# Half of the second layer's weights decoded during the first phase and kept in DRAM; the first batch's x @ w_in by token tile

## The chip, the core and the metric

The kernel runs on one core of a Trainium2 chip. Its engines are TensorE (PE, matmuls; its weight loads stand apart as PEld), VectorE (DVE), ScalarE (ACT), GpSimd (POOL) and SyncE (SP, which here only issues the DMAs). The metric is device microseconds (us) of one execution. Three runs of the kernel before the change took 1190.75, 1192.31 and 1192.62 us, so the median is 1192.31.

## The reference

```python
# attention over 8 batches x 8 heads: 512 tokens and 32 state rows per head, D = 64
scores  = x @ state.T / 8;  a  = softmax(scores);   xread = a @ state
scores2 = state @ x.T / 8;  a2 = softmax(scores2);  sread = a2 @ x
x = concat([xread, sread], tokens)      # heads joined: 8 * (512 + 32) = 4352 rows of 512
# first layer, 512 -> 1024 -> 512
h = x @ w_in;  solu = h * softmax(h)
ln = (solu - mean) / sqrt(var + 1e-6) * g_ln
y = ln @ w_out
# second layer, 512 -> 2048 -> 512
g = relu(y @ w2_in) ** 2
out = g @ w2_out
```

The weights come as float64. The kernel reads them as pairs of 32-bit words and turns each pair into a float32 on the chip. A matmul of full precision is then made of three passes with operands split into a high and a low part (`PASSES`): high x high, high x low, low x high.

## The kernel before, in words

**Two phases.** Phase one takes the eight batches b = 0 to 7 in turn: attention, `x @ w_in`, the SoLU with its layer norm, and `ln @ w_out`, whose result goes to DRAM (`y_d`). After batch 7 the state rows of all batches follow as one group "s" of 256 rows (lines 839 to 844). Phase two reads the `y_d` back group by group (`load_y`) and computes for each of 16 slices m of the 2048 hidden columns a product L3 (`emit_l3`, output `h`), the relu and square (`relu2`), and a product L4 (`emit_l4`, output `o`). L4 of a slice stands two slices behind its L3 (`LAG = 2`).

**What runs ahead.** While PE multiplies batch b by w_out (`emit_l2`, eight slices k, output `y`), it also does attention of batch b + 2 and `x @ w_in` of batch b + 1 (`emit_l1`), placed between the column tiles by the `after` table. For each slice k it transposes the normed tokens (`emit_lnT`, output `lnTp`); ACT and DVE turn them into the high and the low part of `lt` (lines 644 and 647), which the products of that slice read. `emit_lnT` of slice k + 1 stands ahead of the products of slice k.

**Decoding a weight.** `decode` (line 263) makes one 128x512 block of float32 out of 512 KB: a DMA from SP into one of three `raw` buffers, an ACT instruction (Prelu, line 291), two DVE instructions (shift and shift-or, lines 294 and 297) in one of three `dec` buffers, then in `split_w` an ACT cast to the high part (line 241) and a subtraction for the low part on POOL or DVE (line 247). w_in has eight such blocks, w_out eight, and the second layer 32: for each slice m one of w2_in (`wa`) and one of w2_out (`wb`). `load_w2(m)` starts both. Slices 0 to 3 start at k = 4 to 7 of batch 7, slices 4 to 7 at every second k of group "s", slices 8 to 15 at the start of phase two.

**First batch.** w_in is decoded by halves of its columns c = 0, 1. `emit_sw(0, c)` multiplies the state by the half c, and `emit_l1(0, t)` (four token tiles t) needs `sw` of a half for its products of that half. The four tiles are written as generators: the program takes the half c = 0 of all four tiles first, then `emit_sw(0, 1)`, then the half c = 1 of all four (lines 764 to 774).

**What sets the order.** Nothing is reordered on the chip: each engine takes its instructions in the order in which the program emits them. That order comes from `Flow`, a small planner with a clock of its own. Every piece of work off PE is a generator that offers its next step with the engines that may do it, a cost for each and the time from which it is ready; `poll` hands a step out as soon as an engine is free by the planner's costs, the task with the earliest latest-start first. The program is built twice, and the second time the due times that the first found (`plan`) set these priorities.

Of the kernel before, what the change touches and what calls it, by code (L numbers as in the profile page):

```python
# [8 lines left out]
F32 = mybir.dt.float32  # L9
# [139 lines left out]
def attn_solu_relu2_kernel(  # L149
# [58 lines left out]

    y_d = [dram.tile([P, KD, S], F32, name=f"y_d{b}") for b in range(B)]
    y_ds = dram.tile([P, KD, NSR], F32, name="y_ds")  # L210

    wi = [ap_.tile([P, F1], F32, name=f"wi{k}") for k in range(KD)]
    wo = [wp.tile([P, 2, DM], F32R, name=f"wo{k}") for k in range(K1)]
# [11 lines left out]
    def take(name):  # L225
        def ok():
            if room[name]:
                room[name] -= 1
                return True
        return None, 0.0, ok  # L230
# [32 lines left out]
    def decode(dst_h, dst_l, src, pool=None, w=None, spare=False):  # L263

        raw, dec = ("raw2", "dec2") if spare else ("raw", "dec")
        if pool is None:  # L270
            yield take(raw)
            t = (ap_ if spare else raw_p).tile(
                [P, 512, 2], I32, tag=raw, name="raw", bufs=3
            )
        else:
            t = pool.tile([P, 512, 2], I32, tag="u", name="raw_u")
        tf = t.rearrange("p n c -> p (n c)")
        src = src.bitcast(I32)
        if len(src.shape) == 3:
            tf = tf.rearrange("p (k f) -> p k f", k=src.shape[1])  # L280
        f = dma(tf, src, 512)
        own = w is None
        if own:
            yield take(dec)
            w = (ap_ if spare else dec_p).tile(
                [P, 512], F32, tag=dec, name="dec", bufs=2 if spare else 3
            )
        w_i = w.bitcast(I32)
        hi, lo = t[:, :, 1], t[:, :, 0]
        h = hi.bitcast(F32)  # L290
        f = yield {"A": 0.66}, f, lambda e: nc.scalar.activation(
            out=w, in_=h, func=AF.Prelu, scale=2.0 ** -112, alpha=-(2.0 ** 32)
        )
        f = yield {"V": 0.46}, f, lambda e: nc.vector.tensor_scalar(  # L294
            out=w_i, in0=w_i, scalar1=3, scalar2=None, op0=ALU.logical_shift_left
        )
        f = yield {"V": 0.69}, f - fl.HOP, lambda e: nc.vector.scalar_tensor_tensor(  # L297
            out=w_i, in0=lo, scalar=29, in1=w_i, op0=ALU.logical_shift_right, op1=ALU.bitwise_or
        )
        if pool is None:  # L300
            give(raw)
        if not own:
            return f
        f = yield from split_w(dst_h, dst_l, w, f)
        give(dec)
        return f
# [67 lines left out]
    def exp_t(b, g):  # L374


        et = e_T[b, g] = ap_.tile([P, S], F32, tag="eT", name="eT", bufs=1)
        task = done.pop(("nm", b, g))
        s, nm, l = s_sb[b][:, g, :], nms.pop((b, g)), l2[b][:, g:g + 1]

        def gen():
            yield None, 0.0, lambda: task["done"] is not None
            f = yield {"A": 0.82}, task["done"], lambda e: nc.scalar.activation(
                out=et, in_=s, func=AF.Exp, bias=nm, accum_out=l
            )
            return f

        done["eT", b, g] = fl.spawn(gen(), 3.0)
# [44 lines left out]
    def emit_e(b, g):  # L433


        ps = pm.tile([P, T, P], F32, tag="m", name="ep")
        fl.pe(0.11 * T, pm_slot(), done.pop(("eT", b, g)))
        et = e_T.pop((b, g))
        for t in range(T):
            nc.tensor.transpose(ps[:, t, :], et[:, t * P:(t + 1) * P], ident)  # L440
        done["e2", b, g] = one(
            {"A": 0.6, "V": 0.65}, copy(s_sb[b][:, g, :], ps.rearrange("p t q -> p (t q)"))
        )
        pm_free.append(done["e2", b, g])

    def emit_aT(b, g):
        f = fl.need(done["a", b, g])
        if g == 0:
            aT[b] = ap_.tile([P, 2, G, S], F32R, tag="aT", name="aT")
        ps = pm.tile([P, T, P], F32, tag="m", name="aTp")  # L450
        fl.pe(0.11 * T, f, pm_slot())
        for t in range(T):
            nc.tensor.transpose(ps[:, t, :], a_sb[b][:, g, t, :], ident)  # L453
        pf = ps.rearrange("p t q -> p (t q)")
        if b == 0:
            done["aT", b, g] = one({"A": 0.57, "V": 0.6}, copy(aT[b].bitcast(F32)[:, 0, g, :], pf))
        else:
            done["aT", b, g] = split_psum(aT[b][:, 0, g, :], aT[b][:, 1, g, :], pf, 512)
        pm_free.append(done["aT", b, g])
# [158 lines left out]
    def emit_l1(b, t, in_y=False):  # L618
        a, w, passes = aT[b], sw[b], PASSES
        if b == 0:  # L620
            a, w, passes = a.bitcast(F32), w.bitcast(F32), ((0, 0),)
        return solu_ln(b, t, l1_products(
            in_y, [done["aT", b, g] for g in range(G)], lambda c: done["sw", b, c],
            lambda i, k: a[:, i, k, t * P:(t + 1) * P], lambda j, k: w[:, j, k], G, passes,
        ))
# [76 lines left out]
    def phase2_right():  # L702
# [4 lines left out]
        p2["o"] = ctx.enter_context(tc.tile_pool(name="op", bufs=3, **right, **tw))  # L707
        w2_tiles(p2["w"], 0, K2 // 2)

    def load_w2(m):  # L710
        src = w2_in[:, m * P:(m + 1) * P].rearrange("(k p) f -> p k f", p=P)
        done["wa", m] = fl.spawn(decode(wa[m][:, 0], wa[m][:, 1], src))
        done["wb", m] = fl.spawn(decode(wb[m][:, 0], wb[m][:, 1], w2_out[m * P:(m + 1) * P, :]))

    def load_y(j):
        src, n = groups[j]
# [43 lines left out]
    emit_sw(0, 0, True)  # L760
    for g in range(G):
        emit_aT(0, g)
    exp_t(0, 0)
    l1_0 = [emit_l1(0, t, t % 2 == 0) for t in range(T)]
    for i, h in enumerate(l1_0):
        if i % 2:
            emit_e(0, i // 2)
            if i < T - 1:
                exp_t(0, i // 2 + 1)
        if i == T - 1:  # L770
            emit_sw(0, 1, True)
        next(h)
    for h in l1_0:
        next(h)
    sread(0)
    load_xn(1)
    scores(1)
# [6 lines left out]

    emit_lnT(0, 0, T)

    for b in range(B):
        nxt, nn = b + 1 < B, b + 2 < B
        off = 1 if b == 0 else 0
        l1_at = [t + (b < 2) for t in range(T)]  # L790
        if b == 0:
            load_x(2)
        for k in range(K1):
            if k + 1 < K1:
                emit_lnT(b, k + 1, T)
            after = {c: [] for c in range(KD)}
            if b == 0 and k == 0:
                after[1].append(lambda: emit_aT(1, 0))
                after[3].append(lambda: emit_aT(1, 1))
            if b == 0 and k == 1:  # L800
                after[1].append(lambda: sread(b + 1))
                after[3].append(lambda: emit_xs(b + 1))
                if nn:
                    after[1].append(lambda: load_xn(b + 2))
            if nn:
                if k == off + 1:
                    after[1].append(lambda: scores(b + 2))
                    if b + 3 < B:
                        after[3].append(lambda: load_x(b + 3))
                for g in range(G):  # L810
                    if k == off + 3 + g:
                        after[2].append(lambda g=g: emit_e(b + 2, g))
                for g in range(G):
                    if k == off + 2 + g:
                        after[2].append(lambda g=g: (emit_sT(b + 2, g), exp_t(b + 2, g)))
                if k >= 6:
                    after[3].append(lambda: emit_sw(b + 2, k - 6))
                if k >= 6:
                    after[1].append(lambda: emit_aT(b + 2, k - 6))
            if b >= 1 and nxt and k == 0:  # L820
                after[3].append(lambda: emit_xs(b + 1))
            if b == B - 1:
                if k in (0, 2):
                    after[3].append(lambda: run(emit_l1s(k // 2)))
                if k == 3:
                    phase2_right()
                    load_y(0)
                if k >= 4:
                    load_w2(k - 4)
            if k == K1 - 1:  # L830
                after[1].append(lambda: emit_lnT(*((b + 1, 0, T) if nxt else ("s", 0, TS))))
            emit_l2(b, k, T, y_d[b], after)
            if k in l1_at and nxt:
                run(emit_l1(b + 1, l1_at.index(k)))
        if nn:
            sread(b + 2)
            if b + 3 < B:
                load_xn(b + 3)
    for k in range(K1):
        if k + 1 < K1:  # L840
            emit_lnT("s", k + 1, TS)
        emit_l2("s", k, TS, y_ds)
        if k % 2:
            load_w2(4 + k // 2)
    p1.close()


# [131 lines left out]
```

## Time and profile before

| | |
|---|---|
| median of three runs | 1192.31 us |
| the profiled execution | 1192.82 us |
| its span, first to last instruction | 1190.8 us |
| PE busy | 1148.4 us (96%) |
| DVE busy | 546.5 us (46%) |
| ACT busy | 492.6 us (41%) |
| POOL busy | 167.7 us (14%) |
| DMA | 71.22 MB, mean 60 GB/s |
| mean granted clock of TensorE | 0.988 |

The profiled execution takes 2.0 us more than its span, and it is 0.5 us above the median. Times on the rows below count from the start of the span. The shares of busy time are means over stages that differ: the start, up to the first products with w_out at about 60 us; the eight batches, to 411 us; group "s", to 432 us; phase two behind it, whose first 74 us still decode weights.

### The profile page before, as it was taken

The numbers are of one execution on the slowest core, as the hardware profiler recorded it, in microseconds if no ns is written. First come the engines' busy times: TensorE is split into PE (matmuls) and PEld (weight loads), VectorE is DVE, ScalarE is ACT, GpSimd is POOL, SyncE is SP. The second block draws the span as 40 slices with busy tenths as digits, with TensorE's granted clock in tenths as the row PEclk, the third lists the DMA queues.
The fourth block names the chain that finished last, engine by engine and source line by source line (L and its number), as shares of the span: only waits on it lengthen the run. The fifth ranks groups of instructions, "written<-read, shape, count | busy, mean of one in ns | idle before, by whom it ended". The sixth has DMA issues, their size and how long they took to land.

```text
span 1190.8 us, 14915 instructions
## 1 busy us (share of the span) xinstructions
PE 1148.4 (96%) x5992; PEld 912.7 (77%) x5992; DVE 546.5 (46%) x873; ACT 492.6 (41%) x875; POOL 167.7 (14%) x210
## 2 busy tenths in 40 slices
PE   5699999999999988899999999999999999999998
PEld 2377777777777766688888888888888888888887
DVE  6866766766753589723223223233223233232222
ACT  5856766666754566523222223222222232232222
POOL 1521311311322345200000000000000000010000
PEclk9899999999999999899999999999999999999999
DMA  9323032131002366302002011010020020010000
GB/s 361 119 78 114 1 113 78 36 113 72 1 37 89 109 209 198 120 1 71 1 7 65 1 26 45 1 40 32 1 68 4 1 71 1 1 54 1 1 36 18
DMA packets 27701, 71.22 MB, mean 60 GB/s; under 512 B 3312, under 2 KB 12528, under 8 KB 25584
## 3 DMA queue, kind: packets, MB, share of 16 engines
q1 hardware_dynamic: 27632, 70.27, 17.4%
q8 instruction: 47, 0.77, 0.3%
q14 instruction: 22, 0.18, 0.0%
HBM read 52.43 MB, written 17.83 MB: 59 GB/s over the span
## 4 chain that ended last, share of the span: by engine, by line
PE 86%; DVE 6%; DMA 4%; ACT 2%; issue 2%; SPq 0%; ACTq 0%; DVEq 0%
PE o L897 29%; PE h L882 29%; PE y L673 14%; PE hps L612 8%; PE lnTp L638 2%; DMA raw<-w_out 2%; DVE dec L297 1%; DMA raw<-w_in 1%; PE hps L358 1%; DVE dec L294 1%; DMA raw_u<-w_in 1%; PE srd L469 1%; DVE u L577 1%; PE sTp L397 1%; PE aTp L453 1%
## 5 line engine op out<-in xcount | busy, mean ns | idle before, releaser
L897 PE MATMUL o<-wb,g 128*128 128x512 f32 x1632 | 398.9, 392 | 6.8 <-DVE g L247 4.5
L882 PE MATMUL h<-yt,wa 128*128 128x512 f32 (+1 forms) x1728 | 395.3, 378 | 0.0
L897 PEld LDWEIGHTS o<-wb,g 128*128 128x128 f32 x1632 | 306.7, 189 | 73.4 <-DVE g L247 6.9
L882 PEld LDWEIGHTS h<-yt,wa 128*128 128x128 f32 x1728 | 314.5, 189 | 61.6
L866 DVE TENSOR_TENSOR r<-r 128x512 f32<-128x512 f32 (+1 forms) x144 | 109.0, 757 | 386.0 <-ACT r L859 385.8
L859 ACT ACTIVATE r<-h 128x512 f32<-128x512 f32 (+1 forms) x144 | 82.7, 574 | 397.5 <-PE h L882 397.5
L673 PE MATMUL y<-lt,wo 128*128 128x512 f32 (+1 forms) x864 | 221.1, 397 | 8.0 <-DVE lt L647 5.9
L673 PEld LDWEIGHTS y<-lt,wo 128*128 128x128 f32 x864 | 149.8, 190 | 46.6 <-issue 8.4
L247 DVE TENSOR_TENSOR g<-r,g 128x512 fp32r<-128x512 f32 (+1 forms) x144 | 96.3, 669 | 80.8 <-ACT g L241 74.9
L241 ACT CAST g<-r 128x512 fp32r<-128x512 f32 (+1 forms) x144 | 85.8, 596 | 100.2 <-DVE r L866 99.6
L612 PE MATMUL hps<-sw,aT 128*128 128x512 f32 x368 | 97.5, 413 | 0.5 <-ACT sw L241 0.5
L247 POOL TENSOR_TENSOR yt<-yraw,yt 128x1024 fp32r<-128x1024 f32 (+1 forms) x8 | 18.2, 2276 | 551.7 <-ACT yt L241 551.7
L612 PEld LDWEIGHTS hps<-sw,aT 128*128 128x128 f32 x368 | 68.6, 189 | 22.6 <-issue 5.6
L548 DVE TENSOR_REDUCE hm<-hps 128x1 f32<-128x512 f32 x68 | 46.3, 690 | 51.7 <-PE hps L612 46.1
L647 DVE SCALAR_TENSOR_TENSOR lt<-lnTp,g_sb,lt 128x512 fp32r<-128x512 f32 (+1 forms) x72 | 51.6, 718 | 32.5 <-ACT lt L644 31.8
L241 ACT COPY u<-hps 128x512 f32<-128x512 f32 x68 | 39.7, 583 | 62.9 <-DVE hm L548 62.9
L591 POOL TENSOR_SCALAR es<-es 128x1 f32<-128x1 f32 x34 | 30.4, 893 | 191.3 <-ACT e L572 190.3
L644 ACT ACTIVATE lt<-lnTp,g_sb 128x512 fp32r<-128x512 f32 (+1 forms) x72 | 48.3, 673 | 8.2 <-PE lnTp L638 8.2
L577 DVE SCALAR_TENSOR_TENSOR u<-u,e 128x1024 f32<-128x1024 f32 x34 | 46.4, 1365 | 10.3 <-ACT e L572 10.2
L583 ACT ACTIVATE e<-u,nmu 128x1024 f32<-128x1024 f32 x34 | 39.2, 1153 | 20.5 <-DVE nmu L580 20.5
L638 PE MATMUL lnTp<-ident,u 128*128 128x128 f32 x272 | 42.4, 276 | 3.5 <-POOL u L601 2.5
L638 PEld LDWEIGHTS lnTp<-ident,u 128*128 128x128 f32 x272 | 33.4, 142 | 12.0 <-POOL u L601 2.7
(82 smaller groups left out, 714.0 us busy)
## 6 DMA issues: line engine op xcount, KB each, us to landing
raw<-w_out SPq DMA_DIRECT2D x24, 512.0 KB, 4.5
out<-osb SPq DMA_DIRECT2D x34, 256.0 KB, 2.2
xT<-x_t SPq DMA_DIRECT2D x8, 1024.0 KB, 4.8
xn<-x_n SPq DMA_DIRECT2D x8, 1024.0 KB, 5.4
y_d<-ys SPq DMA_DIRECT2D x16, 512.0 KB, 2.7
yraw<-y_d SPq DMA_DIRECT2D x16, 512.0 KB, 5.7
raw<-w_in SPq DMA_DIRECT2D x16, 512.0 KB, 4.1
raw_u<-w_in SPq DMA_DIRECT2D x8, 512.0 KB, 9.5
```

Source lines behind the costliest of these rows:

```text
L241: nc.scalar.copy(out=out, in_=in_)
L247: return lambda e: eng_of[e].tensor_tensor(out=out, in0=in0, in1=in1, op=ALU.subtract)
L577: nc.vector.scalar_tensor_tensor(out=u, in0=u, scalar=1.0, in1=e_, op0=ALU.mult, op1=ALU.mult, accum_out=us)
L612: nc.tensor.matmul(out=ps, lhsT=lhsT(i, k), rhs=rhs(j, k)[:, cs], start=(k == 0 and n == 0), stop=(k == n_k - 1 and n == len(passes) - 1),)
L638: nc.tensor.transpose(ps[:, t, :], u_t[key, t][:, k * P:(k + 1) * P], ident)
L644: f = yield {"A": 0.1 + nt * 0.143}, f, lambda e: nc.scalar.activation(out=o[:, 0], in_=pf, func=AF.Copy, scale=gk)
L647: f = yield {"V": 0.1 + nt * 0.155}, f, lambda e: nc.vector.scalar_tensor_tensor(out=o[:, 1], in0=pf, scalar=gk, in1=o[:, 0].bitcast(F32), ...
L673: nc.tensor.matmul(out=ps, lhsT=wo[k][:, w, c * P:(c + 1) * P], rhs=o[:, a], start=(k == 0 and i == 0), stop=(k == K1 - 1 and i == 2),)
L859: first = one({"A": 0.06 + n / 1000}, lambda e: nc.scalar.activation(out=r, in_=hps, func=AF.Relu))
L866: f = yield {"V": 0.15 + n / 960}, first["done"], lambda e: nc.vector.tensor_tensor(out=r, in0=r, in1=r, op=ALU.mult)
L882: nc.tensor.matmul(out=hps, lhsT=wa[m][:, w, k, :], rhs=yt[j][:, a, k, :], start=(k == 0 and i == 0), stop=(k == KD - 1 and i == 2),)
L897: nc.tensor.matmul(out=ops[j][t], lhsT=g[:, a, t * P:(t + 1) * P], rhs=wb[m][:, w, :], start=(m == 0 and i == 0), stop=(m == K2 - 1 and i ...
```

## The change

There are two edits. First, the 16 blocks of slices 0 to 7 of the second layer are decoded during batches 1 to 6, at k = 0, 3 and 6, into one of three buffers (`w2s`, with the tag of buffers that the decoding of w_out no longer needs) and stored to 16 new DRAM tiles `w2_d`. From k = 4 of batch 7 on, `reload_w2` brings them back with 16 plain DMAs into `wa` and `wb`. The decoding in batch 7 and in group "s" is gone; slices 8 to 15 are decoded where they were. Second, `emit_sw(0, 1)` stands ahead of the first batch's `emit_l1`, and each token tile runs through both halves before the next one starts.

```diff
+    w2_d = [dram.tile([P, 2, 512], F32, name=f"w2_d{i}") for i in range(K2)]
...
+    def early_w2(i):
+        def gen():
+            yield take("raw2")
+            t = ap_.tile([P, 2, 512], F32R, tag="raw2", name="w2s", bufs=3)
+            src = w2_sources(i // 2)[i % 2]
+            th, tl = t[:, 0], t[:, 1]
...
+            yield from decode(th, tl, src)
+            dma(w2_d[i], t.bitcast(F32), 512)
+            give("raw2")
+        done["w2_d", i] = fl.spawn(gen(), 30.0)
+    def reload_w2(m):
+        fl.need([done["w2_d", 2 * m], done["w2_d", 2 * m + 1]])
+        done["wa", m] = dma(wa[m].bitcast(F32).rearrange("p a k f -> p a (k f)"), w2_d[2 * m], 512)
+        done["wb", m] = dma(wb[m].bitcast(F32), w2_d[2 * m + 1], 512)
...
+    emit_sw(0, 1, True)
     exp_t(0, 0)
-    l1_0 = [emit_l1(0, t, t % 2 == 0) for t in range(T)]
-    for i, h in enumerate(l1_0):
-        if i % 2:
-            emit_e(0, i // 2)
-            if i < T - 1:
-                exp_t(0, i // 2 + 1)
-        if i == T - 1:
-            emit_sw(0, 1, True)
-        next(h)
-    for h in l1_0:
-        next(h)
+    for t in range(T):
+        run(emit_l1(0, t, t % 2 == 0))
+        if t % 2:
+            emit_e(0, t // 2)
+            if t < T - 1:
+                exp_t(0, t // 2 + 1)
...
                 if k >= 4:
-                    load_w2(k - 4)
+                    reload_w2(2 * k - 8)
+                    reload_w2(2 * k - 7)
+            if b in range(1, 7) and k % 3 == 0 and early:
+                early_w2(early.pop(0))
...
         emit_l2("s", k, TS, y_ds)
-        if k % 2:
-            load_w2(4 + k // 2)
```

The line numbers of the changed kernel are 2 higher in the functions around the change, and 25 higher in phase two.

PE at the start, before: `aTp` are the transposed attention weights of batch 0, `hps<-sw,aT` the products of `emit_l1`, `hps<-wi` those of `emit_sw`, `ep` transposes for the state read, `srd` the state read.

```order
L453 MATMUL aTp<-ident,a_sb 128x128 x8
L612 MATMUL hps<-sw,aT 128x512 x2
L440 MATMUL ep<-ident,eT 128x128 x4
L612 MATMUL hps<-sw,aT 128x512 x4
L440 MATMUL ep<-ident,eT 128x128 x4
L358 MATMUL hps<-wi_106,bdf 32x512 x2
L358 MATMUL hps<-wi_107,bdf 32x512 x2
L358 MATMUL hps<-wi_108,bdf 32x512 x2
L358 MATMUL hps<-wi_109,bdf 32x512 x2
L612 MATMUL hps<-sw,aT 128x512 x10
L469 MATMUL srd<-xn,s_sb 32x64 x32
```

The same place of PE in the changed kernel:

```order
L455 MATMUL aTp<-ident,a_sb 128x128 x8
L360 MATMUL hps<-wi_122,bdf 32x512 x2
L360 MATMUL hps<-wi_123,bdf 32x512 x2
L360 MATMUL hps<-wi_124,bdf 32x512 x2
L360 MATMUL hps<-wi_125,bdf 32x512 x2
L614 MATMUL hps<-sw,aT 128x512 x8
L442 MATMUL ep<-ident,eT 128x128 x4
L614 MATMUL hps<-sw,aT 128x512 x8
L442 MATMUL ep<-ident,eT 128x128 x4
L471 MATMUL srd<-xn,s_sb 32x64 x32
```

The eight products with the second half of w_in moved ahead of all sixteen products of the four token tiles; before, six of the sixteen stood ahead of them.

DVE in a middle batch, before: from the high and low part of one slice (`lt`) over the lines of attention (`aT`, `sw`) to the next.

```order
L647 SCALAR_TENSOR_TENSOR lt<-lnTp,g_sb,lt 128x512
L601 TENSOR_SCALAR u<-u,nmu,vs 128x1024
L647 SCALAR_TENSOR_TENSOR lt<-lnTp,g_sb,lt 128x512
L601 TENSOR_SCALAR u<-u,nmu,vs 128x1024
L247 TENSOR_TENSOR aT<-aTp,aT 128x512
L247 TENSOR_TENSOR sw<-hps,sw 128x512 x2
L247 TENSOR_TENSOR aT<-aTp,aT 128x512
L647 SCALAR_TENSOR_TENSOR lt<-lnTp,g_sb,lt 128x512
```

The same stretch of DVE in the changed kernel:

```order
L649 SCALAR_TENSOR_TENSOR lt<-lnTp,g_sb,lt 128x512
L603 TENSOR_SCALAR u<-u,nmu,vs 128x1024
L649 SCALAR_TENSOR_TENSOR lt<-lnTp,g_sb,lt 128x512
L249 TENSOR_TENSOR aT<-aTp,aT 128x512
L296 TENSOR_SCALAR dec<-dec 128x512
L299 SCALAR_TENSOR_TENSOR dec<-raw,dec 128x512
L249 TENSOR_TENSOR sw<-hps,sw 128x512 x2
L249 TENSOR_TENSOR aT<-aTp,aT 128x512
L649 SCALAR_TENSOR_TENSOR lt<-lnTp,g_sb,lt 128x512
```

The two instructions of one decode came in ahead of the `sw` and the second `aT`, and one `u` went to POOL.

DVE at the end of group "s" and the start of phase two, before: each 128x256 `lt` of a slice stands behind a decode; `r` and `g` are the square and the low part of `relu2`.

```order
L647 SCALAR_TENSOR_TENSOR lt<-lnTp,g_sb,lt 128x256
L294 TENSOR_SCALAR dec<-dec 128x512
L297 SCALAR_TENSOR_TENSOR dec<-raw,dec 128x512
L647 SCALAR_TENSOR_TENSOR lt<-lnTp,g_sb,lt 128x256
L294 TENSOR_SCALAR dec<-dec 128x512
L297 SCALAR_TENSOR_TENSOR dec<-raw,dec 128x512
L294 TENSOR_SCALAR dec<-dec 128x512
L297 SCALAR_TENSOR_TENSOR dec<-raw,dec 128x512
L294 TENSOR_SCALAR dec<-dec 128x512
L297 SCALAR_TENSOR_TENSOR dec<-raw,dec 128x512
L866 TENSOR_TENSOR r<-r 128x512
```

The same place of DVE in the changed kernel:

```order
L649 SCALAR_TENSOR_TENSOR lt<-lnTp,g_sb,lt 128x256 x8
L891 TENSOR_TENSOR r<-r 128x512
L249 TENSOR_TENSOR g<-r,g 128x512
L296 TENSOR_SCALAR dec<-dec 128x512
L299 SCALAR_TENSOR_TENSOR dec<-raw,dec 128x512
L891 TENSOR_TENSOR r<-r 128x512
L296 TENSOR_SCALAR dec<-dec 128x512
L299 SCALAR_TENSOR_TENSOR dec<-raw,dec 128x512
L249 TENSOR_TENSOR g<-r,g 128x512
```

The eight `lt` of group "s" follow one another with no decode between them, and the decodes of slices 8 to 15 begin behind the first square of phase two.

## Rows read from the trace of the kernel before

**Rows 1.** Windows of stages: length, busy us (instructions) per engine, PEclk, DMA share, GB/s.

```profile
0.00:60.30 60.30, 38.13 (x244) 16.35 (x244) 47.82 (x91) 43.94 (x82) 21.56 (x34) 0.89 0.63 237
...
411.40:431.70 20.30, 14.85 (x112) 13.14 (x111) 15.99 (x23) 13.49 (x28) 10.94 (x8) 1.00 0.68 224
431.70:505.40 73.70, 66.94 (x267) 52.16 (x266) 60.23 (x74) 42.87 (x73) 29.55 (x21) 0.93 0.54 170
505.40:1190.80 685.40, 681.73 (x3097) 567.82 (x3095) 201.80 (x288) 176.40 (x295) 18.18 (x8) 1.00 0.08 24
```

**Rows 2.** Timeline of PE, end of phase one: start, us, what, [idle before it <- releaser].

```profile
388.58 7.03 PE L612 MATMUL hps<-wi,xs 128*128 128x512 f32 x16
...
412.15 1.96 PE L673 MATMUL y<-lt,wo 128*128 128x256 f32 x12 [0.35 <-ACT lt L644]
...
414.09 1.63 PE L673 MATMUL y<-lt,wo 128*128 128x256 f32 x12
...
415.69 1.66 PE L673 MATMUL y<-lt,wo 128*128 128x256 f32 x12
...
431.69 8.34 PE L882 MATMUL h<-yt,wa 128*128 128x512 f32 x36
```

**Rows 3.** Timeline of PE, first part of phase two.

```profile
465.07 2.56 PE L897 MATMUL o<-wb,g 128*128 128x512 f32 x10 [1.37 <-DVE g L247]
...
494.64 4.64 PE L897 MATMUL o<-wb,g 128*128 128x512 f32 x10 [0.61 <-DVE g L247]
...
505.37 0.84 PE L882 MATMUL h<-yt,wa 128*128 128x512 f32 x3
```

**Rows 4.** Chain that ended last, undisturbed phase two: start, us, what.

```profile
502.81 2.72 PE o L897 x12
```

**Rows 5.** Tile dec from 404 to 500 us: shortest/median/longest in ns.

```profile
L291 ACT ACTIVATE dec<-raw x32: 657/668/710, 403.9 to 493.2; 128x512 f32<-128x512 f32 x32
L294 DVE TENSOR_SCALAR dec<-dec x32: 411/422/1523, 405.4 to 494.5; 128x512 int32<-128x512 int32 x32
L297 DVE SCALAR_TENSOR_TENSOR dec<-raw,dec x32: 691/693/1810, 406.1 to 495.0; 128x512 int32<-128x512 int32 x32
L241 ACT CAST wa<-dec x16: 602/619/628, 407.7 to 482.1; 128x512 fp32r<-128x512 f32 x16
...
L247 POOL TENSOR_TENSOR wa<-dec,wa x15: 1286/1410/1803, 408.4 to 481.3; 128x512 fp32r<-128x512 f32 x15
```

**Rows 6.** Timeline of DVE, phase two with decoding.

```profile
453.02 1.78 DVE L866 TENSOR_TENSOR r<-r 128x512 f32<-128x512 f32 x1
...
456.77 0.68 DVE L247 TENSOR_TENSOR g<-r,g 128x512 fp32r<-128x512 f32 x1
...
468.24 1.59 DVE L866 TENSOR_TENSOR r<-r 128x512 f32<-128x512 f32 x1
```

**Rows 7.** Windows: one middle batch, columns as in rows 1.

```profile
190.30:235.60 45.30, 44.57 (x315) 33.98 (x314) 30.74 (x57) 29.36 (x55) 9.95 (x18) 1.00 0.22 75
```

**Rows 8.** Line 647 (low part of lt): shortest/median/longest in ns.

```profile
L647 DVE SCALAR_TENSOR_TENSOR lt<-lnTp,g_sb,lt x72: 472/750/753, 59.5 to 429.9; 128x512 fp32r<-128x512 f32 x64, 128x256 fp32r<-128x256 f32 x8
```

**Rows 9.** Timeline of PE, the one wait of a middle batch.

```profile
222.77 0.66 PE L397 MATMUL sTp<-ident,s_sb 128*128 128x128 f32 x4 [0.73 <-ACT s_sb L241]
```

**Rows 10.** Timeline of PE, the start.

```profile
22.02 2.37 PE L612 MATMUL hps<-sw,aT 128*128 128x512 f32 x4
...
32.15 7.13 PE L612 MATMUL hps<-sw,aT 128*128 128x512 f32 x16 [0.53 <-ACT sw L241]
39.22 1.10 PE L469 MATMUL srd<-xn,s_sb 128*32 128x64 f32 x64
...
60.26 2.08 PE L673 MATMUL y<-lt,wo 128*128 128x512 f32 x4 [2.14 <-DVE lt L647]
```

**Rows 11.** Timeline of ACT, the exponential of the first batch's last token tile.

```profile
48.48 1.14 ACT L572 ACTIVATE e<-u,nmx 128x1024 f32<-128x1024 f32 x1
```

**Rows 12.** Windows: a stretch full of weight loads, columns as in rows 1.

```profile
10.00:20.00 10.00, 5.38 (x24) 1.61 (x23) 9.30 (x20) 6.25 (x11) 1.05 (x1) 0.98 1.02 419
```

More of the change, by code (lines that the diff above doesn't have):

```diff
@@ L708, in phase2_right, with w2_sources @@
         w2_tiles(p2["w"], 0, K2 // 2)
-    def load_w2(m):
-        src = w2_in[:, m * P:(m + 1) * P].rearrange("(k p) f -> p k f", p=P)
-        done["wa", m] = fl.spawn(decode(wa[m][:, 0], wa[m][:, 1], src))
-        done["wb", m] = fl.spawn(decode(wb[m][:, 0], wb[m][:, 1], w2_out[m * P:(m + 1) * P, :]))
+    def w2_sources(m):
+        return (
+            w2_in[:, m * P:(m + 1) * P].rearrange("(k p) f -> p k f", p=P),
+            w2_out[m * P:(m + 1) * P, :],
+        )
+    def load_w2(m):
+        a, b = w2_sources(m)
+        done["wa", m] = fl.spawn(decode(wa[m][:, 0], wa[m][:, 1], a))
+        done["wb", m] = fl.spawn(decode(wb[m][:, 0], wb[m][:, 1], b))
+    def early_w2(i):
[4 more added lines that the diff above has]
+            th, tl = t[:, 0], t[:, 1]
+            if i % 2 == 0:
+                th, tl = (v.rearrange("p (k f) -> p k f", k=KD) for v in (th, tl))
+            yield from decode(th, tl, src)
[6 more added lines that the diff above has]
+        done["wb", m] = dma(wb[m].bitcast(F32), w2_d[2 * m + 1], 512)
     def load_y(j):
@@ L785, in attn_solu_relu2_kernel @@
     emit_lnT(0, 0, T)
+    early = list(range(K2))
     for b in range(B):
```

## The prediction

> **What bounds the kernel now.** I read the windows by stage first. PE sets the time wherever it is busy throughout, so the question for each stage is what PE loses there. Behind 505 us it loses next to nothing: 681.7 of 685.4 us busy at full clock. The losses are in three places [rows 1]: the start, where DVE is busy 47.8 of 60.3 us and PE only 38.1; group "s", where PE is busy 14.9 of 20.3 us; and the first 74 us of phase two, where PE is busy 66.9 us and its granted clock is 0.93 in the mean, between its two levels of 1.2 and 2.4 GHz. In the last two DVE is busy 16.0 of 20.3 and 60.2 of 73.7 us, and the decoding of w2 is what it has there beside its steady work.
>
> Two timelines of PE give these two losses in numbers. In group "s" the second slice starts at 414.09 and the third at 415.69, so an undisturbed slice takes 1.60 us. Seven such steps from the second slice on would end at 414.09 + 7 x 1.60 = 425.29. Phase two starts at 431.69 instead [rows 2]: 6.4 us lost, and 0.35 before the first slice, where `lt` waits on an ACT queue that holds decoding. That is 6.8. In phase two one product of 12 matmuls takes 2.72 us [rows 4]. From 431.69 to 505.37 PE does 264 matmuls (36 at first, then ten products with w2_out and nine with w2_in), 22 x 2.72 = 59.8 us of work in 73.7 us [rows 2, 3]. So 13.8 us are lost there, part of it to waits (1.37, 0.61 us) and part to clock: ten matmuls take 2.56 us behind one wait and 4.64 behind the longer ones near 494 [rows 3]. Both stages together lose 20.6 us.
>
> **Group "s".** The change takes every decode out of batch 7 and group "s", and the eight `lt` follow one another on DVE. The reload takes no time of ACT, DVE or POOL. It is 16 DMAs of 512 KB, 8.4 MB. At the 419 GB/s of a stretch full of loads that is 20 us [rows 12]; at the 224 of group "s" 37 us [rows 1]. The space for it is free when the last products with w_in end, at 388.58 + 7.03 = 395.6 [rows 2], 29 us before phase two would now start (near 424.8), and slice m needs 1 MB every 5.44 us, which is 4.7 us of transfer even at the lower rate. So it is hidden, with slice 0 first in the queue. The stores of `y_d` stand behind it on SP; they are read again only in the last group but one of phase two. The gain is 6.8 us, with 6.4 and 7.1 (eight steps of 1.60 from 411.8 on) as its ends.
>
> **Phase two.** Sixteen blocks are still decoded, and DVE's order has three decodes per slice m, as before. What such a step takes is in the trace: from the square at 453.02 to that at 468.24 there are two steps with three decodes each, 7.61 us a step [rows 6]. PE needs 5.44 us a step. By the shortest durations the step would be 3 x (0.42 + 0.69) + 0.69 + 0.68 = 4.7 us [rows 5, 6], and would fit. The row shows instead that the shift and the shift-or reach 1.52 and 1.81 us while POOL subtracts for 1.41 [rows 5]. The Trainium skill, page "SBUF — State Buffer", section "Who interferes with whom", says that a DVE instruction with two SBUF inputs and a GpSimd instruction that reads SBUF share a port that one of them holds for its whole instruction. By that rule the stretched steps stay, since 14 of the 16 subtractions are again on POOL; the trace agrees. By the shortest durations nothing would be lost in this stage (a rival below).
>
> I replay it with 7.61 us a step. Count from the start S of phase two. The first three products with w2_in end at 2.7, 5.4 and 8.2 us. The first decodes wait for their DMAs (issued about S, landing 4 to 5 us later), so the squares of slices 0 to 2 are hardly held up: slice 2 has its square near 9.5. Then comes the pace of three decodes a step: squares 3, 4, 5 near 16.5, 24.1, 31.7; square 6, with a `yt` subtraction in its step, near 40. The low part `g` is done 4.4 us behind its square (456.77 + 0.68 - 453.02, [rows 6]): 20.9, 28.5, 36.1, 44.4. PE wants them at 24.5, 29.9, 35.4 and 40.8 (slice m at 8.16 + 5.44m). Slices 3 and 4 are in time, slice 5 is late by less than the first two passes of its product, which need the high part alone, and slice 6 by about 3.5 us. Behind it the last decode is done and the delay shrinks. I add 1 us for matmuls at the lower clock behind that wait, so 4.5 of the 13.8 us remain and 9.3 come back. The ends: 13.8, if DVE keeps up, and 13.8 - 11.6 = 2.2, if the 16 decodes cost their whole excess, 16 / 3 x (7.61 - 5.44) = 11.6 us.
>
> **Batches 1 to 6.** Each of 16 early decodes adds ACT 0.67 + 0.62 = 1.29 us, DVE 0.42 + 0.69 = 1.11 us, POOL 1.41 us [rows 5], and on SP two DMAs of 512 KB. That is 2.7 decodes a batch: 3.4 us of ACT and 3.0 of DVE, against 45.3 - 29.4 = 15.9 and 45.3 - 30.7 = 14.6 us that these two have idle [rows 7]. So on the mean they are covered, and what counts is what queues behind a decode. PE waits for `lt` alone with little to spare, and on DVE the decodes stand in the stretches where products of `emit_l1` give PE more to do, and beside `aT` and `sw`; none stands directly between the tight `lt` of the last slices. `lt` itself never stretches: 0.753 us at most in 72 [rows 8]. The one wait that PE has in a batch, 0.73 us for the copy of `ep` on ACT [rows 9], can grow. On SP the store of a decoded block waits for POOL, and the loads of x behind it have most of a batch to spare. Per decode the ends are 0 and 1.29 + 1.11 = 2.40 us, fully exposed; over 16 that is 0 to 38. I take 1.0 us in all, nearest to a wait of 0.73 that grows by a quarter in each of six batches.
>
> **The start.** Before, the products of the first half begin at 22.02, while the second half is still being decoded; the last eight run from 32.15 to 39.22, 0.89 us each (16 records, two to a product) [rows 10]. Now all sixteen stand behind the second half. At the worst they begin where that half's products began before: 32.15 + 16 x 0.89 + 2 x 0.6 for the two `ep` = 47.6, 8.4 us after 39.22. But the exponential of the last tile ran only at 48.48 [rows 11], some 8 us after its product could have allowed it (39.22 plus 1.3 for copy and maximum): ACT and DVE were the queue. Tile by tile they start on tile 0 sooner and end about as late. The other end: one decode (1.11), a multiplication (0.68) and two `sw` subtractions (0.68 each) of DVE move from ahead of the first `lt` to behind it or to POOL, 3.2 us. The read of the state, the scores of batch 1 and their transposes stand behind the products on PE, and these come later by about 5 us of which waits absorb most. I take +0.5, between -3.2 and +8.4, near the row of the queue, which had the room.
>
> **The sum.** -6.8 - 9.3 + 1.0 + 0.5 = -14.6 us. The profiled execution, a span of 1190.8 and 2.0 around it, would be 1178.2. It is 0.5 above the median, so against 1192.31 the forecast is 1177.7.
>
> **The rivals.**
> - *Everything comes back.* DVE keeps up, as the shortest durations say, and start and batches cost nothing: 1192.3 - 20.6 = 1171.7. For it: far fewer decodes stand between the squares. Against it: the measured step of 7.61 us. Chance 0.17.
> - *Decoding paces phase two still.* The excess of 11.6 us is paid in full, and 2.2 instead of 9.3 come back: 1177.7 + 7.1 = 1184.8. For it: the step and the order of three decodes are the same. Against it: PE starts with a lead of two slices and only 16 blocks are left. Chance 0.15.
> - *The start is exposed.* The late products shift the first `y` at 60.26 [rows 10] by all of 8.4 us, and PE's clock, 0.89 there in the mean [rows 1], falls in the gap ahead of them: 1192.3 - 16.1 + 8.4 + 1.0 = 1185.6. Against it: the 8 us of room on ACT. Chance 0.10.
> - *The other side: the early decodes are exposed.* Each stands ahead of an `lt` or of a copy that frees a PSUM buffer, and PE waits it out. From 15.6 / 16 = 0.98 us per decode (6.8 + 9.3 less the 0.5 of the start) the kernel is slower; fully exposed it is 16 x 2.40 = 38.4, so 1192.3 - 15.6 + 38.4 = 1215. For it: PE waits for every `lt`. Against it: two thirds busy engines in those batches, with a single wait of 0.73 us. Chance 0.05.
> - *It doesn't do what it says:* the reload comes too late and phase two waits for `wa`. At 224 GB/s the last of the eight slices would land near 433, 8 us behind S, and it is wanted only some 30 us behind S. Chance 0.02, about 1182.
>
> The forecast has 0.51, and its own range is 1174 to 1182. The range 1170.5 to 1186 takes in the first three rivals. A measurement of this kernel can tell 0.2%, 2.4 us: faster by more than that 0.92, within it 0.04, slower 0.04.
>
> **What would show it.** Right: group "s" in steps of 1.60 us with phase two starting about 13 us or less after its first slice; three decodes a step of about 7.6 us on DVE for slices 3 to 6, and one wait of PE of 2 to 5 us near the seventh product with w2_out; batches of 45.3 to 45.6 us; the first steady `y` within 3 us of 60.3. Wrong: batches 1 to 6 longer than 47 us, the first `y` behind 65 us, or a wait of PE for a `wa` that a DMA brings.

## The result and the profile after

The changed kernel takes 1180.38 us (median of four runs, 1179.18 to 1181.59), the kernel before 1192.46 beside it: ratio 0.9902, interval 0.9885 to 0.9919. The forecast was 1177.7. The profiled execution has a span of 1179.5 us, against 1190.8 before.

Windows of the changed kernel by stage, to be read against [rows 1] (columns as there; group "s" from the same slice on):

```profile
0.00:60.70 60.70, 38.89 (x244) 16.28 (x244) 44.37 (x86) 42.33 (x80) 20.47 (x32) 0.89 0.63 235
416.40:429.10 12.70, 12.70 (x111) 12.66 (x110) 3.48 (x8) 4.73 (x12) 0.00 (x0) 1.00 0.21 84
429.10:500.00 70.90, 68.04 (x293) 55.51 (x292) 49.99 (x62) 36.83 (x62) 19.75 (x14) 0.98 0.45 141
500.00:1179.50 679.50, 675.79 (x3071) 562.88 (x3069) 199.15 (x285) 175.08 (x293) 18.17 (x8) 1.00 0.08 24
```

Group "s" is full: PE is busy all of 12.7 us, DVE has only its eight `lt`. Phase two begins with 2.9 us of idle PE where before it had 6.8. But group "s" begins 5.0 us later than before (416.4 against 411.4): something was lost earlier. The timeline of PE at the three places:

```profile
60.67 2.02 PE L675 MATMUL y<-lt,wo 128*128 128x512 f32 x4 [0.44 <-DVE lt L649]
...
244.16 1.68 PE L360 MATMUL hps<-wi,bdf 64*32 64x512 f32 x16 [0.34 <-DVE sw L249]
...
416.57 1.64 PE L675 MATMUL y<-lt,wo 128*128 128x256 f32 x12
418.18 1.64 PE L675 MATMUL y<-lt,wo 128*128 128x256 f32 x12
...
429.12 8.34 PE L907 MATMUL h<-yt,wa 128*128 128x512 f32 x36
...
472.69 0.73 PE L922 MATMUL o<-wb,g 128*128 128x512 f32 x2 [2.58 <-ACT g L243]
473.70 4.16 PE L922 MATMUL o<-wb,g 128*128 128x512 f32 x10 [0.28 <-DVE g L249]
```

The first steady `y` is 0.4 us later than in [rows 10] (0.3 from batch 1 on). Slices of group "s" follow in 1.61 us with no wait [rows 2]. In phase two there is one wait, at the seventh product with w2_out, where [rows 3] shows waits at several products; the ten matmuls behind it take 4.16 us, and the granted clock is 0.78 from 475 to 480 us. The new row is at 244.16: PE waits for `sw` in the middle of a batch, and the 16 matmuls take 1.68 us, where the same 16 take 1.09 in the kernel before:

```profile
242.32 1.09 PE L358 MATMUL hps<-wi,bdf 64*32 64x512 f32 x16
```

Four differences make up the change of the span, each from the same instruction in both timelines: start +0.3, batches 1 to 6 +4.7, group "s" from its second transposes to phase two 12.68 instead of 20.27, so -7.6, and phase two to the last product 746.67 instead of 755.44, so -8.8. Sum -11.4; the span differs by 11.3.

**Where the batches lose it.** Here are four queues of the changed kernel around that wait. SP comes first:

```profile
236.78 0.33 SPq L225 DMA_DIRECT2D w_d<-w2s  x1
237.20 0.39 SPq L225 DMA_DIRECT2D raw<-w_in  x1
```

POOL, whose subtraction the store on SP waits for:

```profile
234.94 0.55 POOL L600 TENSOR_TENSOR vs<-vs,mhalf 128x1 f32<-128x1 f32 x1
235.46 1.29 POOL L249 TENSOR_TENSOR w2s<-dec,w2s 128x512 fp32r<-128x512 f32 x1
```

ACT and DVE:

```profile
241.63 0.69 ACT L293 ACTIVATE dec<-raw 128x512 f32<-128x512 f32 x1 [3.47 <-DMA raw<-w_in]
242.22 1.06 ACT L243 CAST sw<-hps 128x512 fp32r<-128x512 f32 x2
```

```profile
242.35 0.43 DVE L296 TENSOR_SCALAR dec<-dec 128x512 int32<-128x512 int32 x1 [3.46 <-ACT dec L293]
243.42 1.28 DVE L249 TENSOR_TENSOR sw<-hps,sw 128x512 fp32r<-128x512 f32 x2
```

ACT at the same place of the kernel before:

```profile
238.61 1.08 ACT L241 CAST sw<-hps 128x512 fp32r<-128x512 f32 x2 [1.88 <-PE hps L358]
```

Read from the top: the subtraction runs at 235.46 behind the layer norm's small operations. SP issues its store only then, at 236.78, and the load of the next raw block, which needs none of this, goes out behind it at 237.20. It lands some 4.4 us later. Until then ACT stands idle at this block's Prelu for 3.47 us, with the two `sw` casts behind it, and DVE stands at its shift for 3.46. The PSUM buffers of `sw` come free late, and PE loses 0.34 us of waiting and 0.59 of longer matmuls at 244.16. In the kernel before, the casts of `sw` ran 2.5 us earlier in the batch: 15.8 us behind the second `sTp` there, and 18.3 behind it here. Measured from the second `sTp` of one batch to that of the next, batches 1 and 2 lose nothing; batches 3 to 6 lose 0.9, 1.3, 1.0 and 1.5 us.

### The profile page after: what moved, and what is told of

It reads as the page before. It is cut to its first block, busy times and chain, and to the rows that moved or that the text cites. A ratio compares the mean times of both kernels' runs of the same rounds, so it can differ in the third digit from the quotient of the medians.

```text
span 1179.5 us, 14989 instructions
## 1 busy us (share of the span) xinstructions
PE 1145.5 (97%) x5992; PEld 910.7 (77%) x5992; DVE 534.7 (45%) x866; ACT 490.9 (42%) x875; POOL 177.8 (15%) x217
## 4 chain that ended last, share of the span: by engine, by line
PE 90%; DVE 4%; ACT 3%; DMA 2%; issue 1%; SPq 0%; POOL 0%; ACTq 0%; DVEq 0%; POOLq 0%
PE o L922 31%; PE h L907 31%; PE y L675 14%; PE hps L614 8%; PE lnTp L640 2%; PE hps L360 1%; DMA raw<-w_in 1%; DMA raw_u<-w_in 1%; PE sTp L399 1%; DVE dec L299 1%; PE srd L471 1%; DVE hm L550 1%; ACT e L585 1%; DVE dec L296 1%; PE aTp L455 0%
## 5 line engine op out<-in xcount | busy, mean ns | idle before, releaser
L614 PEld LDWEIGHTS hps<-sw,aT 128*128 128x128 f32 x368 | 69.0, 189 | 23.6 <-issue 6.8
L579 DVE SCALAR_TENSOR_TENSOR u<-u,e 128x1024 f32<-128x1024 f32 x34 | 42.5, 1251 | 9.9 <-ACT e L574 9.9
L585 ACT ACTIVATE e<-u,nmu 128x1024 f32<-128x1024 f32 x34 | 39.2, 1152 | 15.8 <-DVE nmu L582 14.9
L574 ACT ACTIVATE e<-u,nmx 128x1024 f32<-128x1024 f32 x34 | 39.1, 1150 | 3.0 <-DVE nmx L567 2.9
```

Of the source, the lines that this page charges most:

```text
L585: f = yield {"A": 1.16}, f, lambda e: nc.scalar.activation(out=e_, in_=u, func=AF.Square, bias=nmu, accum_out=vs)
L614: nc.tensor.matmul(out=ps, lhsT=lhsT(i, k), rhs=rhs(j, k)[:, cs], start=(k == 0 and n == 0), stop=(k == n_k - 1 and n == len(passes) - 1),)
```

## The experiments

Stages of each kernel from its PE timeline: the second `sTp` of batch 1 (start), from there to phase two, and from there to the end of the last product. The loss of the batches is the middle column less 333.95, which is the 341.54 of before without the 7.59 of group "s" (12.68 to 12.69 us from its second transposes in every kernel with the early decodes). Each row of stages is one profile. Ratios, with their intervals, are to the kernel before as it ran beside each (medians 1190.84 to 1192.46).

| kernel | start | to phase two (loss of the batches) | phase two | median us | ratio |
|---|---|---|---|---|---|
| before | 90.15 | 341.54 | 755.44 | 1192.46 | 1 |
| changed | 90.43 | 338.69 (4.7) | 746.67 | 1180.38 | 0.9902 [0.9885, 0.9919] |
| e1 early decodes only | 91.51 | 339.21 (5.3) | 747.96 | 1183.58 | 0.9934 [0.9922, 0.9947] |
| e2 order of the first batch only | 90.15 | 341.35 | 753.08 | 1189.96 | 0.9988 [0.9980, 0.9997] |
| e3 store behind load | 89.85 | 335.88 (1.9) | 748.55 | 1178.75 | 0.9891 [0.9876, 0.9907] |
| e4 decodes spread | 89.50 | 338.94 (5.0) | 746.37 | 1181.85 | 0.9917 [0.9903, 0.9932] |
| e6 subtraction on DVE in phase two | 90.81 | 338.69 (4.7) | 741.62 | 1176.81 | 0.9878 [0.9864, 0.9891] |
| e7 late y | 90.29 | 338.66 (4.7) | 748.76 | 1182.34 | 0.9926 [0.9912, 0.9940] |
| e8 = e3 + e7 | 89.30 | 335.22 (1.3) | 748.68 | 1179.61 | 0.9900 [0.9886, 0.9913] |
| e9 = e3 + e7 + e4 | 89.76 | 335.36 (1.4) | 743.55 | 1174.46 | 0.9862 [0.9848, 0.9876] |
| e10 = e3 + e6 | 88.95 | 335.48 (1.5) | 741.62 | 1173.18 | 0.9854 [0.9838, 0.9871] |
| e11 = e3 + e6 + e4 | 87.81 | 335.80 (1.9) | 741.61 | 1172.22 | 0.9846 [0.9832, 0.9861] |
| e12 all subtractions on DVE | 88.12 | 334.83 (0.9) | 741.62 | 1171.50 | 0.9839 [0.9825, 0.9854] |
| e13 = e3 + e12 | 90.27 | 337.33 (3.4) | 741.61 | 1173.54 | 0.9858 [0.9843, 0.9872] |

**The two edits apart.** e1 is the changed kernel with the first batch in its old order, e2 the kernel before with the new order alone.

> The early decoding with its stores and reloads, but the first batch's products in their old order (by halves of the columns). Theory (the new order of the first batch costs its 0.3 us and nothing else hangs on it): 0.3 us less than the changed kernel, 1180.1 us, ratio to the kernel before 0.9897, and the first batch's attention steady at about 60.3 us again. Rival (the two edits need each other, the new order keeps VectorE and ScalarE free for the first decodes): slower than the changed kernel by over 1 us, with the extra in batch 1.

> The kernel before with the new order of the first batch's products alone, all of the second layer's weights decoded where they were. Theory: 1192.7 us, 0.3 above the kernel before, not to be told from it; ratio 1.000. Rival (the new order has a gain of its own, up to the 3.2 us that the prediction left open below): 1189.3 to 1191.5, with a first steady attention block before 60 us.

In e1 the theory fell: it is slower than the changed kernel, by 0.3% in the ratios and 2.9 us in the spans (1.1 by batch 1, 0.5 in the batches, 1.3 in phase two). The direction is the rival's. Its reason is not shown: the first steady `y` stands at 60.7 in both, and what follows it differs by the clock (the next `y` of six matmuls takes 2.91 us in e1 and 2.08 in the changed kernel, with a granted clock of 0.50 and 0.80 from 63 to 66 us). The 1.3 us of phase two are no sign of it either: in the first 90 us of that phase DVE, ACT and POOL have the same instructions in the same order in e1, e3 and the changed kernel, and it takes 747.96, 748.55 and 746.67 us. In e2 the median is 0.1% better, but the profile has the start where it was, 90.15, and the gain of 2.4 us in phase two, whose instructions the edit leaves in the same order too. So without the early decodes the new order gives nothing that the trace can tell from scatter; with them the kernel is 0.3% faster, for a reason that stays open.

**The store on SP.** The raw load goes out ahead of the store of the block before:

```diff
+        if loaded:
+            loaded()
...
+    kept = []
+    def store_last():
+        for i, t in kept:
+            dma(w2_d[i], t.bitcast(F32), 512)
...
-            yield from decode(th, tl, src)
-            dma(w2_d[i], t.bitcast(F32), 512)
-            give("raw2")
+            yield from decode(th, tl, src, loaded=store_last)
+            kept.append((i, t))
...
```

> The changed kernel, but SP issues the load of each next raw block before the store of the block decoded before it, so that no load stands behind a store that waits for POOL. Theory (the 4.75 us of batches 1 to 6 come from that order: load late, ScalarE's decode waits 3.5 us with the casts of sw behind it, TensorE waits for their PSUM buffer): the loss in the batches falls from 4.75 to at most 1 us, 1176 us (1175.5 to 1177.0), ratio 0.9865, and no decode of ScalarE between 66 and 386 us waits over 2 us for raw<-w_in. Rival (POOL's subtractions, 1.3 us each among the layer-norm's operations, stretch VectorE and hold the chain, wherever the load stands): the loss stays over 4 us, 1180 us.

The loss fell from 4.7 to 1.9 us, not to at most 1: most of it was this order. What ACT's decodes wait for a raw block between 66 and 386 us (total, times, longest), in the changed kernel:

```profile
ACT dec L293 <- DMA raw<-w_in: 10.7, 5, 3.7
ACT dec L293 <- DMA raw<-w_out: 7.4, 3, 3.1
```

and with the load ahead of the store:

```profile
ACT dec L295 <- DMA raw<-w_in: 5.6, 3, 2.6
ACT dec L295 <- DMA raw<-w_out: 2.3, 2, 1.8
```

18.1 us became 7.9; one wait of 2.6 us stayed, where I expected none over 2. Set beside the kernel before by the transposes within the batch shown, the changed kernel is 0.3 us late from the third `lnTp` on and 1.3 from the state read on; e3 has the 0.3 still and the other 1.0 no longer. At that place a Prelu of a decode stands on ACT ahead of a copy and of the `lt`, a loss of the kind that the prediction did price; no run takes this Prelu away. The time fell by less than the batches gave, and the profile has phase two 1.9 us longer. Its instructions stand in the same order as in the changed kernel, and by as much the stage scatters (below), so nothing shows it to be a cost of the edit.

**What paces phase two.** Three edits: e4 starts the decodes of slices 8 to 15 one slice a step, e7 loads the next group's y from slice 10 on, e6 takes the decodes' subtraction off POOL.

```diff
-    for m in range(K2 // 2, K2):
-        load_w2(m)
...
+            if i < K2 // 2:
+                load_w2(K2 // 2 + i)
```

```diff
-            if m == 2 and j + 1 < len(groups):
+            if m == 10 and j + 1 < len(groups):
```

```diff
-        f = yield {"P": 1.25, "V": 0.69}, f, sub(dst_l, v, dst_h.bitcast(F32))
+        f = yield {"V": 0.69} if "late" in done else {"P": 1.25, "V": 0.69}, f, sub(dst_l, v, dst_h.bitcast(F32))
...
+    done["late"] = True
     for m in range(K2 // 2, K2):
```

> The changed kernel, but the decodes of slices 8 to 15 start one slice a step in the first eight steps of phase two and not all together ahead of it. Theory (the decodes pile up ahead of the relu, square and multiply of the first slices, and the seventh product with w2_out waits 2.6 and 0.3 us and then runs 2 us at the lower clock): wait and lower clock go, 24 products from the start of phase two take 65.3 to 66 us and not 70.35, 1175.5 us (1175.2 to 1176.5), ratio 0.986. Rival (each decode beside POOL's subtraction is too slow by itself, however they are spaced): a wait of the same size at the same place or some steps later, 1179 to 1181 us.

> The changed kernel, but the y of the next group is loaded and split from slice 10 on and not from slice 2 on, behind the last decode. Theory (the wait at the seventh product with w2_out comes from that load: it waits for a buffer of the decodes' ring, lands late, and ScalarE's cast and VectorE's subtraction of yt stand in order ahead of the square of slice 6): no wait over 0.5 us there, full clock behind it, the 24 products take 65.3 to 66.3 us and not 70.35, ratio 0.987 (0.9865 to 0.988). Rival (the pace of three decodes a step, 7.1 to 7.65 us against 5.44, is what makes the square late, with or without yt): a wait of 1.5 to 3 us at the seventh or eighth product stays, ratio 0.989 to 0.9905.

> The changed kernel, but in phase two the decodes' subtractions run on VectorE alone, none on POOL. Theory (POOL's subtraction holds VectorE's shift and shift-or back while it runs): those two take 0.42 and 0.69 us everywhere in phase two and never 1.5 to 1.8; the extra subtraction of 0.68 us per decode is cheaper than the stretch, three decodes and a slice's square and subtraction take 6.7 to 6.9 us and not 7.1 to 7.65, and the loss of 5.1 us in the first 24 products falls by 1 to 3 us: ratio to the kernel before 0.988 to 0.9895 (the changed kernel 0.9902). Rival (the stretch has another cause, or VectorE's total counts): the durations stay, or the steps get longer than 7.65 us and the loss grows by 2 us or more, ratio 0.992.

e4's theory fell: the wait split in two, and phase two was as long (746.37 against 746.67). e7's fell too. PE with the late y:

```profile
472.39 0.73 PE L922 MATMUL o<-wb,g 128*128 128x512 f32 x2 [2.41 <-ACT g L243]
474.37 4.63 PE L922 MATMUL o<-wb,g 128*128 128x512 f32 x10 [1.24 <-DVE g L249]
```

The same product waits no less, 3.7 us in all: in the place of `yt` a fourth decode stands between the squares of slices 5 and 6, where there were three. e6's theory held beyond its numbers. Groups of DVE by shape from 424 to 500 us (busy, mean ns | idle before), the changed kernel:

```profile
L299 DVE SCALAR_TENSOR_TENSOR dec<-raw,dec 128x512 int32<-128x512 int32 x16 | 15.9, 996 | 0.5
L891 DVE TENSOR_TENSOR r<-r 128x512 f32<-128x512 f32 x13 | 14.9, 1147 | 15.4 <-ACT r L884 15.3
L296 DVE TENSOR_SCALAR dec<-dec 128x512 int32<-128x512 int32 x16 | 8.9, 555 | 0.1
L249 DVE TENSOR_TENSOR wa<-dec,wa 128x512 fp32r<-128x512 f32 x2 | 1.4, 680 | 0.0
```

and e6:

```profile
L299 DVE SCALAR_TENSOR_TENSOR dec<-raw,dec 128x512 int32<-128x512 int32 x16 | 10.9, 689 | 0.3
L891 DVE TENSOR_TENSOR r<-r 128x512 f32<-128x512 f32 x14 | 9.6, 686 | 13.9 <-ACT r L884 13.9
L296 DVE TENSOR_SCALAR dec<-dec 128x512 int32<-128x512 int32 x16 | 6.8, 423 | 2.7 <-ACT dec L293 2.7
L249 DVE TENSOR_TENSOR wb<-dec,wb 128x512 fp32r<-128x512 f32 x8 | 5.5, 687 | 1.8 <-ACT wb L243 1.6
L249 DVE TENSOR_TENSOR wa<-dec,wa 128x512 fp32r<-128x512 f32 x8 | 5.5, 687 | 1.3 <-ACT wa L243 1.3
```

With 14 subtractions more, 9.6 us of work, DVE is busy less (47.8 us from 420 to 500, against 52.4): shift, shift-or and square are back at 0.42, 0.69 and 0.69 us, 13.0 us less than at the means of the changed kernel (16 x 0.31 + 16 x 0.13 + 13 x 0.46). In the changed kernel the shift and the shift-or hardly wait (0.1 and 0.5 us in all), and of the squares of slices 0 to 6 only the first does, so there it was DVE's own pace that made the squares late. In e6 no product waits, the granted clock is 1.00, and phase two takes 741.62 us, the same to 0.01 in the five kernels that have this edit. That is the floor of this order of products, 13.8 us under the kernel before, as much as the prediction read as lost there.

**Both places together.**

> Load before store on SP in the batches, and the late y, together. Theory (both causes, and they add): phase two starts some 3 us sooner than in the changed kernel and loses under 1.3 us, ratio 0.9845 (0.984 to 0.986), faster than either alone. Rival (what the batches give is lost again in phase two, as with load before store alone, where it lost 1.9 us more): ratio of the late y alone, 0.987.

> As the kernel with load before store and the late y, and the decodes of slices 8 to 15 start one slice a step. Theory (two decodes a step take about 5.4 us, as much as PE needs, so nothing waits in either order): the same time as without the spreading within 1 us, ratio 0.9845. Rival (spread decodes are late for the slices they serve or stretch over more of the squares): waits of 1 us and more at three or more products, ratio 0.987 or above.

> Load before store on SP in the batches, and the decodes' subtractions of phase two on VectorE alone, together. Theory (the two causes are apart, and what either gives stays): phase two starts 2.8 to 3.5 us sooner than in the changed kernel, and no product with w2_out waits: 1173.3 us, ratio 0.985 (0.9842 to 0.9858), faster than either alone. Rival (as with the late y, what the batches give is lost again in phase two): the ratio of VectorE alone, 0.9878.

> As the kernel before it, and the decodes of slices 8 to 15 start one slice a step. Theory (phase two waits for nothing any more, so its order of decodes gives nothing): the same time within 1 us, ratio 0.985. Rival (two decodes a step, 2 x 1.79 + 1.37 = 4.95 us of VectorE against 5.44 of TensorE, leave squares late where yt comes in between): waits of 1 us, ratio 0.986 to 0.987.

e8's theory fell where e7's did: phase two takes 748.68 us, as long as in e7 (748.76). Its rival did not hold either, since e8 keeps what the batches give: 3.4 us by the stages, and 0.9900 against e7's 0.9926 in the ratios. e9 loses only 1.9 us in phase two, with one wait of 1.14 us, while e4 and e7, each alone, gave nothing; I had expected nothing of the pair. With two decodes a step and no `yt` between them the squares of slices 5 to 7 of e9 follow 5.6 and 5.7 us apart, near PE's 5.44; in e4, with a `yt` in each of the steps to slices 5 and 6, they are 7.6 and 7.2 apart. The pair was not run without e3. e10 is as its theory had it (0.9854, expected 0.985), and e11 is the same within the intervals. So the two losses are apart and add: e10 is faster than e6, as e8 is than e7, by about what the batches give.

**POOL out of the early decodes too.** e12 extends e6's edit to the early blocks, e13 adds e3's order.

> The changed kernel, SP's order as it was, but the decodes' subtractions of all second-layer blocks on VectorE, the early ones in the batches too. Theory (in the batches the store on SP waits for POOL's subtraction, which stands in POOL's queue behind the layer-norm's operations; on VectorE it ends sooner, and the next load goes out sooner): the loss of 4.75 us in batches 1 to 6 falls to under 2.5, ratio 0.9855 (0.985 to 0.987). Rival 1 (where the subtraction runs is no matter, the load stands behind the store either way): the loss stays 4 to 5 us, 0.9878. Rival 2 (16 more subtractions of 0.68 us on VectorE hold up the copies that TensorE waits for): the loss grows by over 1.5 us, 0.989 or above.

> Both in the batches: load before store on SP, and the early subtractions on VectorE; phase two with VectorE alone as well. Theory (with the load ahead of the store nobody waits for the early subtraction, so moving it to VectorE gives nothing): the time of the kernel with POOL in the batches within 1 us, ratio 0.985. Rival (POOL's subtraction beside VectorE stretches VectorE's operations in the batches too, which is what is left of the loss there): faster by another 1 to 1.5 us, ratio 0.984, with batches of 45.3 us.

e12 has the lowest median, 0.9839, with an interval that overlaps those of e10 and e11. It loses 0.9 us in the batches with SP's order untouched, but not for the reason I gave. ACT of e12, at the place of the rows of ACT above:

```profile
236.84 1.08 ACT L243 CAST sw<-hps 128x512 fp32r<-128x512 f32 x2 [1.89 <-PE hps L360]
...
241.72 1.07 ACT L243 CAST sw<-hps 128x512 fp32r<-128x512 f32 x2 [0.49 <-PE hps L360]
242.68 0.69 ACT L293 ACTIVATE dec<-raw 128x512 f32<-128x512 f32 x1
```

and its PE:

```profile
240.54 1.09 PE L360 MATMUL hps<-wi,bdf 64*32 64x512 f32 x16
```

Its store goes out only 0.6 us sooner in the batch (12.3 us behind the second `sTp`, against 12.9), so the load is hardly earlier. But the planner, with another cost for the subtraction, put this Prelu behind the `sw` casts, which no longer wait for the load. e3 makes the load early, and e12 puts the decode where a late load does no harm: either breaks the chain, so the loss needs both halves, the late load and the order on ACT.

e13 has the time of e10 within 1 us in the median, as its theory said. Its profile loses 3.4 us in the batches, with PE waiting up to 1.22 us for the copy of `ep` where it waited 0.73 [rows 9]. ACT and DVE of e13 in batch 1, ahead of that longest wait:

```profile
116.64 0.66 ACT L295 ACTIVATE dec<-raw 128x512 f32<-128x512 f32 x1 [3.21 <-DMA raw<-w_in]
121.50 0.59 ACT L243 COPY u<-hps 128x512 f32<-128x512 f32 x1 [0.61 <-DVE hm L552]
```

```profile
120.19 0.68 DVE L249 TENSOR_TENSOR w2s<-dec,w2s 128x512 fp32r<-128x512 f32 x1
120.79 0.68 DVE L552 TENSOR_REDUCE hm<-hps 128x1 f32<-128x512 f32 x1
```

The early subtraction now stands on DVE ahead of the row maximum `hm` that ACT's copy of `u` waits for, 0.61 us that e10 does not have there. The raw block also came later: ACT waits 3.21 us for it, against 2.56 in e10 and 2.48 in e12. ACT reaches the copy of `ep` without the 0.56 us of idle time that it has in e10. In e12 the same subtraction stands at the same place, and PE's wait grows at one batch only (1.14 us). So the second rival of e12 holds in part: the subtractions on DVE use up time that ACT has to spare. Why the block, issued at the same moment of the batch in the three kernels, lands later in e13 stays open.

## Why the prediction was right, and where it was not

The time lay 2.7 us above the forecast, inside its own range. By terms:

- **Group "s": -6.8, measured -7.6.** The slices do follow in 1.61 us, and the reload is hidden: no product waits for `wa` or `wb`. Most of the rest is the first slice. I counted only its wait of 0.35 us; it also ran 1.96 us instead of 1.64, and it began 0.73 us behind its transposes at 411.42, where it is 0.13 now [rows 2].
- **Phase two: -9.3, measured -8.8.** The replay at 7.61 us a step holds: it put the squares of slices 3 to 6 at 16.5, 24.1, 31.7 and 40 us behind the start; they run at 16.5, 23.6, 31.3 and 41.1. The one wait stands at the product it named, 2.9 us instead of 3.5, and the lower clock costs 2.2 instead of 1, so two smaller errors cancel in part. That the term came out within 0.5 us is luck as well: with the same order of instructions this stage took 746.67 to 748.55 us in three kernels, and 755.44 and 753.08 in the kernel before and e2. The cause that it gave for the long step, POOL's subtraction, is shown by e6; e7 shows that the `yt` in the step of slice 6, which it also named, is not what counts. The prediction quoted the Trainium skill, page "SBUF — State Buffer", section "Who interferes with whom". The trace agrees with that rule: shift-or and square, with two inputs each, stretch to 1.67 and 1.80 us in the changed kernel and not at all in e6. The shift has one SBUF input, and its stretch to 1.52 us is not in the half of the rule that the prediction quoted. The same section of the Trainium skill says that DVE in its two-port modes contends with GpSimd as well. The shift's 0.42 us throughout e6 agrees with that; that the shift runs in such a mode, no run shows.
- **Batches 1 to 6: +1.0, measured +4.7.** This is the step that was mis-sized, and with it failed a sign that the prediction named for being right: batches 3 to 5 take 46.1 to 46.6 us, not 45.3 to 45.6. The prediction looked on SP only for the loads of x behind a store that waits for POOL. Right behind it stood the early decoding's own next load, ACT waited for that in order, and the `sw` casts behind it on ACT were on PE's path. It had noted that the decodes on DVE stand beside `aT` and `sw`, and priced it with a wait of 0.73 us that grows by a quarter [rows 9]. That wait is 0.73 us in every batch of the changed kernel; PE loses the time at other places. The 0.3 to 0.4 us that are left in e3 in each of batches 3 to 6 are of the size priced, and with 0.6 us in batch 2 they make its 1.9. The other 2.8 are the chain shown by e3 and, by another way, e12.
- **Start: +0.5, measured +0.3 in the profile.** Kernels with the same first 60 us differ by more than that (below), so the trace says no more than that none of the 8.4 us of the upper end came.

The rival of exposed early decodes had the right place with the wrong price: 4.7 us over 16 decodes is 0.3 each, under the 0.98 from which it decides. "Everything comes back" was out of reach by the batches and by POOL; e12, which takes nearly all of both away, comes to 1171.5 beside a kernel before at 1190.84, which is 1173.1 on the 1192.31 of the prediction.

## What to carry to other kernels

When a change adds a store that waits for a computation, look at what is behind it on the issuing queue, at who waits for that load in order, and at what stands behind that waiter: the loss appears three queues from its cause. Before work is moved off a busy engine to a free one, compare the busy engine's durations with and without the other at work: here taking 14 subtractions back onto VectorE made VectorE less busy. And two edits that each give nothing can help together: phase two takes 743.55 us with the spread decodes and the late y, against 746.37 and 748.76 with one of them. A theory about a pile-up is therefore not settled by one of them.

## What the runs showed of the hardware that was not expected

The start scatters more than a small term. With the same program for the first batch, the second `sTp` of batch 1 stands at 88.12, 89.50, 90.29, 90.43 and 90.81 us in the profiles of e12, e4, e7, the changed kernel and e6. The granted clock between 30 and 62 us is 0.89, 0.90, 0.93, 0.93 and 0.87 there, so the mean clock alone does not order them. Behind it the stages repeat where PE has hardly a wait. With the same order of instructions on DVE, ACT and POOL the batches take 338.66 to 338.94 us (the changed kernel, e4, e6, e7) and 335.22 to 335.88 (e3, e8, e9, e10, e11), and phase two without a wait takes 741.61 or 741.62. Phase two with waits does not repeat: the same order took 746.67, 747.96 and 748.55 us, and 755.44 and 753.08. A difference of one or two microseconds between two profiles is read from a stage that repeats, not from the span.
